# A recurrent token-mixing layer and a gated feed-forward layer in one kernel: the mixing products on four 64x64 quadrants, the first gate products before normalisation, and a written-out program order

## The chip, the cores and the metric

The kernel runs on one core of a Trainium2 chip. TensorE (PE) multiplies matrices, VectorE (DVE), ScalarE (ACT) and GpSimd (POOL) work on tiles, SyncE (SP) issues the DMAs. The metric is the device time of one execution in microseconds; the profile adds what each engine did, in time from the start of the span. In the profile an fp32 matmul stands as two records, each with its weight load (PEld), so a program's 32 matmuls are 64 records.

## The reference, cut to what matters

```python
batch, n_heads, seq, head_dim = (4, 8, 768, 48)
for t in range(S):
    cur = np.einsum('bhd,bhe->bhde', u[None] * kt, vt)
    y[:, :, t] = np.einsum('bhd,bhde->bhe', rt, state + cur)
    state = w[None, :, :, None] * state + np.einsum('bhd,bhe->bhde', kt, vt)
x = y.transpose(0, 2, 1, 3).reshape(3072, 384)
rms = np.sqrt(np.mean(x * x, axis=-1, keepdims=True) + 1e-06)
xn = x / rms * rms_g
g = xn @ w_gate                  # 384 x 1536
silu = g * (1.0 / (1.0 + np.exp(-g)))
out = silu * (xn @ w_val) @ w_out
```

All is fp32 on the chip; the three weight matrices arrive as float64 and are rounded to fp32 by the kernel itself.

## The kernel before

The sequence is cut into 12 chunks of 64 steps (`NS`, `L`); a chunk has 4 batches of 64 steps, 256 tokens. Each chunk goes through `mixing(s)`, which turns the recurrence into products, and then through the feed-forward layer.

`mixing(s)` has these steps, and the names are those of the operations that it records. R and K multiply r and k by powers of w (tables `up`, `down`). A forms the 64x64 scores of k against r for 16 pairs of batch and head (`products`). d and m put the bonus u on the diagonal and the upper triangle of the scores over it, into two tiles ME and MO. Y forms the outputs (`outputs`): the weights are a tile VS that holds 64 rows of v and 64 rows of state one above the other, so each Y matmul sums over 128 rows and fills 64 columns. sq, r, ms, pow, inv, diag, spread and x divide by the root of the mean square: squares, their sum over PE, the root, and a multiplication into `xa`; xb is a copy of `xa` with its two halves of partitions exchanged. U forms the next state (`states`): 32 matmuls over 128 rows, of which 64 hold the decay on a diagonal, so that the old state is decayed by the same matmul; the weights have 48 columns. Four copies per chunk (E on ACT) bring the state back into VS.

For chunk 0 the bonus comes from a product of its own (E, on a tile ku) and k is turned by PE (T), since its token-major copy is not loaded. Its last two heads reach their place in `yT` by four small DMAs (move), as in all chunks.

The feed-forward layer has a first stage for chunks 0 and 1, in cells `g` (gate and value products of 12 records) and `P` (second product), while the weights still arrive: every piece is loaded by SP, taken apart by ACT (ulp) and DVE (bits1, bits2) and added on POOL (sum). From chunk 2 on two chunks are done together by sums of tokens and weights, seven products f1 to f7 per group, six groups, then P1 to P7.

Nothing is issued as it is written. `add` records each operation with its engine, a cost and the keys that it reads and writes in a `Plan`; `search` tries goals with a random generator, `schedule` puts the operations in an order by due times, and `give` issues them in that order, so each engine's queue is that list, in order. Between PE operations of the first 27 us `give` fills idle stretches of the plan with matmuls on a tile of ones (`warm`). PSUM has three double banks a, b, c for the feed-forward layer and two banks `at` for the mixing.

Of the kernel before, what the change touches and what calls it, by code (L numbers as in the profile page):

```python
# [50 lines left out]
P = 128  # L51
# [31 lines left out]

class InOrder:
# [10 lines left out]
class Plan:  # L95
# [5 lines left out]
    AHEAD = 30.0  # L101
    URGENT = 3
    KEEP = 2.0

    def __init__(self):
        self.ops, self.then, self.last, self.readers, self.urgent = [], [], {}, {}, set()
# [22 lines left out]
    def schedule(self, goals, free, count, relaxed, patience=0.3):  # L129

        if len(self.then) < len(self.ops):
            self.then = [[] for _ in self.ops]
            for i, op in enumerate(self.ops):
                for d in op[2]:
                    self.then[d].append((i, self.hop(d, i)))
        late = [goals.get(i, 1e6 + i) for i in range(len(self.ops))]
        early = min(goals[i] for i in goals if i >= relaxed) - self.AHEAD
        for i in reversed(range(len(self.ops))):  # L140
            by, cost = 2 if i >= relaxed else 1, self.ops[i][1]
            for j, hop in self.then[i]:
                due = late[j] - by * (hop + cost)
                if i < relaxed <= j and due < early:
                    due = early
                if due < late[i]:
                    late[i] = due
            if i in self.urgent:
                late[i] -= self.URGENT
        n, then = count, self.then  # L150
        free, port = dict(free), {"DVE": 0.0, "POOL": 0.0}
        missing, mode = [len(op[2]) for op in self.ops[0:n]], None
        at, ready, start, end = [0.0] * n, {e: set() for e in free}, [0.0] * n, [0.0] * n
        for i in range(n):
            if not missing[i]:
                ready[self.ops[i][0]].add(i)
        for _ in range(n):
            when, e = min((max(free[e], min(at[i] for i in ready[e])), e) for e in free if ready[e])
            turn = (lambda i: late[i] + self.KEEP * (self.ops[i][7] != mode)) if e == "PE" else late.__getitem__
            i = min((i for i in ready[e] if at[i] <= when), key=turn)  # L160
            sooner = [j for j in ready[e] if at[j] <= when + patience and turn(j) < turn(i) - 1]
            if sooner:
                i = min(sooner, key=turn)
            s = max(when, at[i])
            if e == "PE":
                s += self.SWITCH * (self.ops[i][7] != mode)
                mode = self.ops[i][7]
            if self.ops[i][5]:
                s = max(s, port["POOL" if e == "DVE" else "DVE"])
            ready[e].remove(i)  # L170
            start[i], end[i] = s, s + self.ops[i][1]
            free[e] = end[i]
            if self.ops[i][5]:
                port[e] = end[i]
            for j, hop in then[i]:
                if j < n:
                    at[j] = max(at[j], end[i] + hop)
                    missing[j] -= 1
                    if not missing[j]:
                        ready[self.ops[j][0]].add(j)  # L180
        return start

    def replay(self, start, free):

        free, port, end, mode = dict(free), {"DVE": 0.0, "POOL": 0.0}, [0.0] * len(start), None
        for i in sorted(range(len(start)), key=lambda i: (start[i], i)):
            e, cost, deps, _, _, locks, _, rows = self.ops[i]
            s = max([free[e]] + [end[d] + self.hop(d, i) + (1.0 if self.ops[d][0] == "SP" else 0.02) for d in deps])
# [5 lines left out]
            free[e] = end[i] = s + cost * (1.0 if e == "PE" else 1.02)  # L194
            if locks:
                port[e] = end[i]
        return end

    def goals_of(self, cells, first, slower):

        goals, t = {}, first
        for i in cells:
            goals[i] = t
            t += self.ops[i][1] * slower
        return goals

    def search(self, cells, first, free, count, relaxed, trials):


        found, last = [], [i for i in range(count) if self.ops[i][0] == "PE"]  # L210
        for seed in range(4):
            rng, best, goals = random.Random(seed), None, dict(first)
            for trial in range(trials):
                new = dict(goals)
                if trial and rng.random() < 0.5:
                    a, by = rng.randrange(len(cells)), rng.uniform(-15, 15)
                    for i in cells[a : a + 1 + int(rng.expovariate(1 / 6))]:
                        new[i] += by
                elif trial:
                    new[rng.randrange(relaxed)] = rng.uniform(0, goals[cells[-1]])  # L220
                end = self.replay(self.schedule(new, free, count, relaxed), free)
                end = max(end[i] for i in last) + 0.3 * sum(end[i] for i in last) / len(last)
                if best is None or end <= best:
                    best, goals = end, new
            found.append((best, seed, goals))
        return min(found)[2]

    def give(self, start, idle=None):

        self.start, busy = start, 0.0  # L230
        for i in sorted(range(len(self.ops)), key=lambda i: (start[i], i)):
# [8 lines left out]
def fast(ctx, tc, chan, tok, vpad, wka, wkb, wot, cols, u_row, out, bad):  # L240
# [27 lines left out]
    col = c_tile([P, 3 * HP], "col")  # L268
    sp.dma_start(out=col, in_=cols)
    wraw, ucol, gcol = col[:, 0:HP], col[:, HP : 2 * HP], col[:, 2 * HP :]  # L270
# [4 lines left out]
    act.activation(spare, eps, AF.Sqrt)  # L275
# [5 lines left out]
    pw = raws.tile([P, HP, L], FP32, name="pw")  # L281
# [3 lines left out]
    VS = c_tile([P, 2, B, VC], "VS")  # L285
    ME = c_tile([P, B, HP, L], "ME")
    MO = c_tile([P, B, HP, L], "MO")
    KH = c_tile([P, 2, B, HP, D], "KH")
# [14 lines left out]

    pool.memset(VS[0:64, 0], 0.0)
    pool.memset(VS[64:128, 1], 0.0)
    pool.memset(KH[32:64, 0], 0.0)
    pool.memset(KH[96:128, 1], 0.0)


    wcol = c_tile([P, HP], "wcol")  # L310
    winv = c_tile([P, HP], "winv")
# [81 lines left out]
    def piece(p, dst, src, key, lo, size):  # L393
# [38 lines left out]
        )  # L432


    du_of = {}

    def crossed_r(s):

        if s:
            return CH[:, 0, 2:4]  # L440
# [1296 lines left out]
```

## Time and profile before

| what | us |
|---|---|
| three runs, median | 625.6 |
| lowest, highest | 619.77, 626.07 |
| profiled execution, its own time | 621.0 |
| its span | 619.3 |
| first gate product starts | 30.62 |
| last matmul ends | 612.14 |

The span runs from the first to the last instruction of the profiled execution; 1.7 us of its time lie outside. The last 7.2 us of the span, from the last matmul on, are the last addition, its store and the end of the program. Since every operation is issued through one helper, all rows have the line L92, and rows are told apart by the names of their tiles.

### The profile page before, as it was taken

The page shows a single profiled execution, that of the slowest core. Times are in us where ns is not written, and L with a number is a line of the kernel's source. Part 1 is how long each engine was busy: PE and PEld are TensorE (multiplying, and loading weights), DVE is VectorE, ACT ScalarE, POOL GpSimd, SP SyncE. Part 2 cuts the span into 40 slices and gives each one's busy share as a digit, 9 for nine tenths or more (in the row PEclk, how much of TensorE's full clock was granted, in tenths as well). Part 3 has the DMA queues.
Part 4 walks back from the last instruction along what each step waited for, and adds up shares of the span by engine and source line. Part 5 has one row for each costly group of instructions (what it writes and reads, how often), then busy time and mean ns, then how long its engine had stood idle before and what let it go on. Part 6 is the DMA issues. An engine that isn't in the chain of part 4 may idle for free.

```text
span 619.3 us, 15403 instructions
## 1 busy us (share of the span) xinstructions
PE 602.3 (97%) x6552; PEld 528.7 (85%) x6552; DVE 443.0 (72%) x632; ACT 365.6 (59%) x933; POOL 43.5 (7%) x41
## 2 busy tenths in 40 slices
PE   7989999999999999999999999999999999999994
PEld 7967777776888899888899888899788899888994
DVE  7698887889887986547887457997555976555631
ACT  5895779558489493345974944874845685232200
POOL 3234322400000000000000000000000000000000
PEclk9899999999999999999999999999999999999998
DMA  8757563213724202325131324231333311310001
GB/s 281 258 197 287 163 215 117 71 58 76 231 58 138 70 8 51 103 78 180 41 121 40 100 85 154 81 119 35 78 103 99 115 35 33 77 52 1 1 14 44
DMA packets 22782, 63.02 MB, mean 102 GB/s; under 512 B 3152, under 2 KB 10160, under 8 KB 21296
## 3 DMA queue, kind: packets, MB, share of 16 engines
q1 hardware_dynamic: 22112, 61.56, 31.9%
q8 instruction: 53, 0.87, 0.6%
q10 hardware_dynamic: 592, 0.39, 0.2%
q14 instruction: 25, 0.20, 0.1%
HBM read 56.04 MB, written 4.72 MB: 98 GB/s over the span
## 4 chain that ended last, share of the span: by engine, by line
PE 92%; DVE 3%; issue 2%; ACT 1%; POOL 0%; ACTq 0%; POOLq 0%; DVEq 0%
PE bank_b L92 31%; PE bank_a L92 27%; PE bank_c L92 24%; PE at L92 10%; DVE bits L92 1%; DVE rows_out L92 1%; DVE ms L92 0%; DVE chan L92 0%; DVE gv L92 0%; ACT ME L92 0%; DVE du L92 0%; DVE t L92 0%; ACT m L92 0%; POOL wb L92 0%; DVE sq L92 0%
## 5 line engine op out<-in xcount | busy, mean ns | idle before, releaser
L92 DVE TENSOR_TENSOR gv<-bank_b,m 128x512 f32<-128x512 f32 x90 | 62.1, 690 | 63.4 <-PE bank_b L92 61.0
L92 ACT ACTIVATE gv<-gv 128x512 f32<-128x512 f32 (+1 forms) x60 | 30.7, 521 | 44.2 <-DVE gv L92 43.7
L92 PE MATMUL bank_b<-xa,wa 64*128 64x256 f32 x444 | 55.7, 383 | 0.9 <-DVE gv L92 0.9
L92 ACT ACTIVATE ME<-dmask,du 64x64 f32<-64x64 f32 x176 | 46.0, 331 | 16.8 <-DVE du L92 16.0
L92 DVE TENSOR_TENSOR gv<-bank_c,gv 128x512 f32<-128x512 f32 x60 | 41.4, 690 | 14.3 <-PE bank_c L92 12.9
L92 PE MATMUL bank_a<-wo,h 128*128 128x192 f32 (+1 forms) x264 | 50.8, 346 | 0.0
L92 ACT ACTIVATE gv<-bank_a 128x256 f32<-128x256 f32 x30 | 11.5, 382 | 66.1 <-PE bank_a L92 66.1
L92 PE MATMUL bank_a<-xa,wa 64*128 64x256 f32 x396 | 49.8, 384 | 0.0
L92 PEld LDWEIGHTS bank_b<-xa,wa 64*128 64x128 f32 x444 | 41.7, 187 | 9.1 <-DVE gv L92 2.4
L92 PE MATMUL bank_a<-xb,wb 64*128 64x256 f32 x396 | 48.9, 379 | 0.0
L92 PEld LDWEIGHTS bank_a<-wo,h 128*128 128x128 f32 x264 | 43.1, 190 | 5.4 <-issue 2.3
L92 ACT ACTIVATE MO<-dmask,du 64x64 f32<-64x64 f32 x176 | 46.8, 339 | 0.8
L92 PE MATMUL bank_c<-t,s 64*128 64x256 f32 x360 | 44.2, 378 | 1.0 <-DVE rows_out L92 1.0
L92 PE MATMUL bank_b<-t,wb 64*128 64x256 f32 x360 | 44.7, 381 | 0.2 <-DVE gv L92 0.2
L92 ACT ACTIVATE rows_out<-rows_out 128x384 f32<-128x384 f32 x72 | 40.1, 558 | 6.6 <-DVE s L92 3.5
L92 PE MATMUL bank_b<-t,s 64*128 64x256 f32 x360 | 44.0, 377 | 0.0
L92 PE MATMUL bank_c<-xb,s 64*128 64x256 f32 x360 | 43.9, 376 | 0.0
L92 PEld LDWEIGHTS bank_a<-xa,wa 64*128 64x128 f32 x396 | 37.1, 187 | 6.9 <-issue 1.4
L92 PEld LDWEIGHTS bank_a<-xb,wb 64*128 64x128 f32 x396 | 37.8, 187 | 4.5
L92 PEld LDWEIGHTS bank_c<-t,s 64*128 64x128 f32 x360 | 34.6, 187 | 6.2 <-DVE rows_out L92 1.8
L92 PEld LDWEIGHTS bank_b<-t,s 64*128 64x128 f32 x360 | 34.8, 187 | 4.3 <-DVE t L92 0.3
L92 PEld LDWEIGHTS bank_c<-xb,s 64*128 64x128 f32 x360 | 34.9, 187 | 4.0
(163 smaller groups left out, 1247.0 us busy)
## 6 DMA issues: line engine op xcount, KB each, us to landing
chan<-in_chan_dram SPq DMA_DIRECT2D x11, 1024.0 KB, 6.0
TOK<-in_tok_dram SPq DMA_DIRECT2D x11, 768.0 KB, 5.3
VS<-in_vpad_dram SPq DMA_DIRECT2D x24, 256.0 KB, 4.0
raw<-in_wot_dram SPq DMA_DIRECT2D x8, 576.0 KB, 4.7
rows_out<-in_wka_dram SPq DMA_DIRECT2D x12, 384.0 KB, 3.2
rows_out<-in_wkb_dram SPq DMA_DIRECT2D x12, 384.0 KB, 3.1
rows_out<-in_wot_dram SPq DMA_DIRECT2D x12, 384.0 KB, 3.4
out_dram<-rows_out SPq DMA_DIRECT2D x43, 96.0 KB, 2.3
```

Of the source, the lines that this page charges most:

```text
L92: return lambda *args, **kwargs: self.tc.keep_in_program_order(give(*args, **kwargs))
```

## The change

Four things change.

- Mixing products. ME, MO and VS go. One tile MT holds the scores, V holds v alone, ST the state alone, RR and RX the decayed r and a copy of it with its halves exchanged for two batches. Y is now 32 matmuls of V against MT and 32 of ST against RR or RX, added up in PSUM; each works on 64 rows and 64 columns, and four that follow each other name four different quadrants. U is 32 matmuls on quadrants, with 64 columns of KH as weights (16 of them the next head's or padding) against 48 columns of v. The state is decayed on ACT by 8 multiplications per chunk and the new part added on DVE (`decay_state`, `keep_states`). d and m work on all 128 partitions at once. The two `at` banks are one tile of two banks.
- The first chunk. E, A and Y go in halves of 16 matmuls (Y: 24); the last two heads are computed straight into their places (`first_outputs`), so the four DMAs go. The six gate products of the first cell take yT and its exchanged copy yb, not divided by the root, and DVE multiplies their result by the reciprocal root from `rms` (`gv 0`). The root comes from POOL, not from ACT's table, so ACT has one table for this stretch. Chunk 0 has no T; half of its K is on POOL; its token-major k is loaded instead. Chunk 1 gets its bonus by E too.
- Tables. `up` and the token table move from DVE to ACT, the tables of powers are twice as wide.
- Order. `search`, `schedule` and their random generator go; a list `ORDER` of 1,526 numbers says in which order the operations are issued. `warm` fills the time before the first E alone, by 9 matmuls of 512 columns.

```diff
+ORDER = [
+    0, 5, 1, 14, 9, 4, 6, 49, 3, 16, 2, 19, 54, 11, 8, 17, 15, 12, 50, 51, 53, 24, 55, 10, 57, 52, 20, 56, 59, 29, 84,
...
-    def give(self, start, idle=None):
+    def give(self, order, free, idle):
...
+        for i in order:
             if self.ops[i][0] == "PE":
-                if idle:
-                    idle(busy, start[i])
+                idle(busy, start[i])
...
+    def products(place, qs, ks, rs):
+        for q in qs:
             for p in range(HP):
+                for h in range(2):
+                    b = 2 * q + h
+                    for z in range(2):
+                        a, c = 64 * (z ^ q), 64 * (1 ^ z ^ h)
+                        pe.matmul(
+                            place(q, h)[c : c + 64, p, :], ks[a : a + D, b, p, :], rs[a : a + D, b, p, :], start=True,
...
+    def first_outputs(tile, q):
+        for p in range(CC):
+            for head, cols in ((HP - 1, L), (p, D)):
+                for h in range(2):
...
-                        py[64 * z : 64 * z + 64, p, bl * L : (bl + 1) * L], VS[:, e, b, p * L : (p + 1) * L],
-                        (ME, MO)[e][:, b, p, :], start=True, stop=True, skip_group_check=True,
...
+                            place(b)[64 * z : 64 * z + 64, p, :], V[c : c + 64, b, p * L : (p + 1) * L],
+                            MT[c : c + 64, b, p, :], start=b < 2 and p == 0, stop=False, skip_group_check=True,
...
+                            place(b)[64 * z : 64 * z + D, p, :], ST[c : c + D, b, p, :], decayed[c : c + D, p, :],
+                            start=False, stop=True, skip_group_check=True,
...
-                    vh = VS[:, z, b, p * L : p * L + D]
-                    pe.matmul(
-                        pu[64 * z : 64 * z + D, bl, p, :], KH[:, z, b, p, :], vh, start=True, stop=True,
...
+                        c, a, x = 64 * (1 ^ z ^ h), 64 * (z ^ q), (b * HP + p) * D
+                        vh = V[c : c + 64, b, p * L : p * L + D]
+                        pe.matmul(
+                            pu[a : a + 64, q, p, :], KH[c : c + 64, x : x + L], vh, start=True, stop=True,
...
+    def decay_state(h):
+        for p in range(HP):
+            x, part = (1 - h) * HP + p, free_dims(ST[:, h, p], (2 * HP * D, 2), (1, D))
+            act.mul(part, part, pows[L][:, x : x + 1])
+
+    def keep_states(s, tile, x):
...
+            if s:
+                dve.tensor_add(to, pu, to)
+            else:
+                act.copy(to, pu)
...
+            lambda: product(ps_, wa[i][:, o], yT if first else xa[s], True), name=f"g {s} {i} {o}", rows=True,
...
+            lambda: product(ps_, wb[i][:, o], yb if first else xb[s], False), name=f"g {s} {i} {o}", rows=True,
...
+        if first:
+            gv, gv_keys = first_gv(o), [f"h{j // 4}.{j % 4}" for j in (15 + 2 * o, 16 + 2 * o)]
+            add(
+                "DVE", 0.72, keys + ["diag"], gv_keys, lambda: dve.tensor_mul(gv, ps_[:, :, 0:NT], free_dims(rms, (0, 2), (1, NT))),
...
-        if until < 27:
-            for _ in range(int((until - since - 0.3) / (0.22 if since else 0.5))):
-                pe.matmul(bank_of["c"][:, 0, 0:P], ones, ones, start=True, stop=True)
+        if until < 9:
+            for _ in range(int((until - since - 0.6) / 0.9)):
+                pe.matmul(bank_of["b"][:, 0], ones, free_dims(ones, (0, 4), (1, P)), start=True, stop=True)
```

How the order changes is shown at three places. On PE, the head of the program before: 15 matmuls of ones, then the bonus product of chunk 0 (bank_a from chan and ku), more ones, and the first scores.

```order
L92 MATMUL bank_c<-ones 128x128 x15
L92 MATMUL bank_a<-chan,ku 64x64 x32
L92 MATMUL bank_c<-ones 128x128 x2
L92 MATMUL at_149<-sq,chan 64x64 x16
L92 MATMUL at_150<-ME,chan 64x64
```

And the head of PE's queue now: the ones are wider, and the halves of the bonus product (ku) and of the scores (RR) alternate, with the first outputs (MT against V) behind them.

```order
L166 MATMUL bank_b<-ones 128x512 x9
L166 MATMUL bank_c<-chan,ku 64x64 x16
L166 MATMUL at<-RR,chan 64x64 x16
L166 MATMUL bank_b<-chan,ku 64x64 x16
L166 MATMUL bank_a<-RR,chan 64x64 x16
L166 MATMUL at<-MT,V 64x64 x4
```

The ones now stand in front of the first bonus product in one piece, and nothing fills PE between the later steps of chunk 0. On PE again, before, the stretch that ends with the first gate products (from xa and wa, xb and wb); the diag row spreads the root and the VS, KH rows are U of chunk 0.

```order
L92 MATMUL bank_c<-ones 128x128 x16
L92 MATMUL at_150<-diag,ones 128x256
L92 MATMUL at_149<-VS,KH 48x48 x16
L92 MATMUL at_150<-VS,KH 48x48 x16
L92 MATMUL bank_b<-xa_145,wa_120 128x256 x6
L92 MATMUL bank_b<-xb_146,wb_124 128x256 x6
L92 MATMUL at_149<-ident,rows_out 128x128 x4
```

The same stretch now; h stands for the exchanged copy yb, which lies in that tile.

```order
L166 MATMUL at<-ones,sq 128x1 x6
L166 MATMUL at<-ident,rows_out 128x128 x4
L166 MATMUL bank_a<-yT,wa_119 128x256 x6
L166 MATMUL bank_b<-yT,wa_119 128x256 x6
L166 MATMUL at<-diag,ones 128x256
L166 MATMUL bank_b<-h,wb_123 128x256 x6
L166 MATMUL bank_a<-h,wb_123 128x256 x6
L166 MATMUL at<-V,KH 64x48 x32
L166 MATMUL bank_a<-chan,ku 64x64 x32
```

Four gate products, and with them the table product (ident), now stand ahead of U of chunk 0; two of them stand ahead of the spread of the root. On DVE, before, the steps d (TENSOR_TENSOR with dmask) and m (COPY_PREDICATED) of chunk 0.

```order
L92 TENSOR_TENSOR chan<-chan,down 128x512 x2
L92 TENSOR_TENSOR ME<-bank_a,dmask 64x512
L92 TENSOR_TENSOR MO<-bank_a,dmask 64x512
L92 TENSOR_TENSOR ME<-bank_a,dmask 64x512
L92 TENSOR_TENSOR MO<-bank_a,dmask 64x512
L92 COPY_PREDICATED ME<-mask,at_150 64x512
L92 COPY_PREDICATED MO<-mask,at_150 64x512
L92 COPY_PREDICATED ME<-mask,at_149 64x512
L92 COPY_PREDICATED MO<-mask,at_149 64x512
```

And now, with the work on weight pieces (bits from raw) behind it:

```order
L166 TENSOR_TENSOR RR<-chan,up 128x512 x2
L166 TENSOR_TENSOR MT<-bank_c,dmask 128x256 x2
L166 COPY_PREDICATED MT<-mask,at 128x256 x2
L166 TENSOR_TENSOR MT<-bank_b,dmask 128x256 x2
L166 COPY_PREDICATED MT<-mask,bank_a 128x256 x2
L166 TENSOR_SCALAR bits_139<-raw_133 128x384
```

The eight instructions on half the partitions became eight of half the length on all partitions, and the first half's mask now stands ahead of the second half's diagonal.

More of the change, by code (lines that the diff above doesn't have):

```diff
@@ L28 @@
-import random
 from collections import deque
@@ L127, in hop @@
         return self.ops[before][4] + (self.HOP if a != b or a == "SP" else 0.0)
[L129 to L181, printed above, removed]
@@ L193, in replay @@
                 mode = rows
[L194 removed]
+            start[i], free[e], end[i] = s, s + cost, s + cost
             if locks:
                 port[e] = end[i]
[L197 to L226, printed above, removed]
[L228 to L231 removed]
+        return start
+    def give(self, order, free, idle):
+        assert sorted(order) == list(range(len(self.ops)))
+        start, busy = self.times(order, free), 0.0
+        for i in order:
             if self.ops[i][0] == "PE":
[L233 to L234 removed]
+                idle(busy, start[i])
                 busy = start[i] + self.ops[i][1]
```

607 lines of the change are left out of this document (301 added, 306 removed), and 70 rows, old and new, of the table ORDER.

## The prediction

> **What bounds the kernel now.** First the page: which engine is full, and what the chain that ended last consists of.
>
> ```profile
> PE 602.3 (97%) x6552; PEld 528.7 (85%) x6552; DVE 443.0 (72%) x632; ACT 365.6 (59%) x933; POOL 43.5 (7%) x41
> PE 92%; DVE 3%; issue 2%; ACT 1%; POOL 0%; ACTq 0%; POOLq 0%; DVEq 0%
> ```
>
> PE is busy for 97% of the span and makes up 92% of the chain. But busy is not useful: before the first gate product PE multiplies ones. So next comes a table by stages: two stretches of the start, the first stage, one steady pair of chunks, the last pair. The columns after the length are the busy time of each engine with its records, the granted clock, and the DMA engines' share and rate.
>
> ```profile
> core 0: us, PE busy (x) PEld busy (x) DVE busy (x) ACT busy (x) POOL busy (x), PEclk, DMA share, GB/s
> 6.83:13.65 6.82, 6.35 (x194) 5.93 (x194) 6.66 (x15) 5.63 (x15) 0.00 (x0) 1.00 1.03 295
> 17.07:20.49 3.42, 3.42 (x47) 3.19 (x47) 3.32 (x5) 1.32 (x4) 0.00 (x0) 0.50 0.88 329
> 30.62:144.63 114.01, 110.48 (x1202) 85.19 (x1198) 98.34 (x130) 82.14 (x213) 34.83 (x23) 1.00 0.45 152
> 337.17:432.99 95.82, 94.85 (x1061) 84.82 (x1060) 68.77 (x94) 61.83 (x160) 0.00 (x0) 1.00 0.32 94
> 528.80:612.14 83.34, 82.55 (x675) 76.03 (x674) 41.70 (x65) 17.45 (x38) 0.00 (x0) 1.00 0.12 33
> ```
>
> From 30.62 on PE hardly rests, at full clock, and in a steady pair DVE and ACT have 27 and 34 us to spare. So two things are worth time: PE's own work after 30.62, and the 30.62 us before it, where DVE is full (6.66 of 6.82) and PE waits.
>
> The timeline of PE in a steady pair gives the prices, from start to next start; a row is start, length, engine, line, operation, out<-in, shapes, count.
>
> ```profile
> 378.13 1.64 PE L92 MATMUL at<-VS,KH 128*48 128x48 f32 x64
> 379.71 1.57 PE L92 MATMUL bank_b<-xa,wa 64*128 64x256 f32 x12
> 381.11 1.46 PE L92 MATMUL bank_c<-t,s 64*128 64x256 f32 x12
> 382.50 0.27 PE L92 MATMUL at<-ME,chan 48*64 48x64 f32 x1
> 383.59 1.57 PE L92 MATMUL bank_a<-xb,wb 64*128 64x256 f32 x12
> 384.99 1.46 PE L92 MATMUL bank_b<-t,wb 64*128 64x256 f32 x12
> 386.28 1.46 PE L92 MATMUL bank_c<-xb,s 64*128 64x256 f32 x12
> 387.68 0.27 PE L92 MATMUL at<-ME,VS 128*64 128x64 f32 x1
> 389.69 1.57 PE L92 MATMUL bank_a<-xa,wa 64*128 64x256 f32 x12
> ```
>
> A gate product between its like takes 1.29 (384.99 to 386.28). The same product ahead of a mixing step takes 1.39 (381.11), behind one 1.40 (379.71). U takes 1.58, A 1.09, Y 2.01. A names four quadrants in turn, and its records step like this (the first and last of 15 such rows in chunk 1):
>
> ```profile
> 37.52 0.22 PE L92 MATMUL at<-ME,chan 48*64 48x64 f32 x1
> 38.34 0.22 PE L92 MATMUL at<-ME,chan 48*64 48x64 f32 x1
> ```
>
> 14 steps in 0.82, so 0.058 for four records. A is 16 x 0.058 = 0.93 of multiplying; its insertion costs 1.09 + 0.10 + 0.11 = 1.30; the other 0.37 are two changes of tile shape, 0.19 each.
>
> **The change, part by part.** Y. Before: 64 records, two at a time on column halves, 2.01. Now 128 records with the shape of A's, 64 columns of weights and 64 of tokens: 32 x 0.058 = 1.86, plus what A has over its steps (1.09 - 0.93 = 0.16): 2.02. I take no change. The upper end is no overlap beyond two, 64 x 0.058 = 3.71, or 1.7 more; the lower end is nothing, since no row has quadrants denser than A's.
>
> U. Before: 1.58 + 0.21 - 0.37 = 1.42 of multiplying, 32 pairs at 0.044. Now 64 records on four quadrants, 48 columns of tokens as before, but weights of 64 columns. The rows of weight loads:
>
> ```profile
> L92 PEld LDWEIGHTS at<-VS,KH 128*48 128x48 f32 x704 | 16.8, 125 | 4.0 <-issue 3.6 <-DVE xa L92 0.3
> L92 PEld LDWEIGHTS at<-chan 48*64 48x64 f32 x352 | 11.1, 134 | 0.0
> L92 PEld LDWEIGHTS bank_b<-KH,chan 48*64 48x64 f32 x64 | 1.9, 135 | 1.7 <-issue 1.7
> ```
>
> The third is T of chunk 0, with just this shape, and its loads are as long as A's (134). So U becomes 16 x 0.058 = 0.93, or by its 48 columns 16 x 0.044 = 0.70. I take 0.93: a gain of 0.49 per chunk, 4.9 for the ten U after the first gate product, up to 7.2.
>
> Changes of shape. Counted in the two programs from the first gate product on, PE changes between row pairs, whole array, column halves and quadrants 100 times before and 84 times now, since Y and U share A's shape and the new order lays mixing steps beside P more often: 16 x 0.19 = 3.0 less.
>
> The start, whose rows are these (fill, slow and fast; bonus product; d and m on DVE; first Y; move; yT, sq, ulp, one addition and one sum of a weight piece as prices; x; first gate product):
>
> ```profile
> 1.14 6.31 PE L92 MATMUL bank_c<-ones 128*128 128x128 f32 x30 [1.14 <-DVE pw L92]
> 24.46 3.82 PE L92 MATMUL bank_c<-ones 128*128 128x128 f32 x32
> 7.72 1.91 PE L92 MATMUL bank_a<-chan,ku 48*64 48x64 f32 x64 [0.27 <-DMA chan<-in_chan_dram]
> 11.05 0.70 DVE L92 TENSOR_TENSOR ME<-bank_a,dmask 64x512 f32<-64x512 f32 x1
> 16.21 0.73 DVE L92 COPY_PREDICATED MO<-mask,at 64x512 f32<-64x512 int32 x1
> 18.30 0.37 PE L92 MATMUL at<-ME,VS 128*64 128x64 f32 x1
> 21.52 2.71 SPq L92 DMA_DIRECT2D yT<-last_heads  x4
> 21.84 0.91 ACT L92 ACTIVATE yT<-at,col 128x128 f32<-128x128 f32 x3
> 21.36 0.61 ACT L92 ACTIVATE sq<-at 128x512 f32<-128x512 f32 x1
> L92 ACT ACTIVATE ulp<-raw 128x384 int32<-128x384 uint32 x6 | 3.2, 548 | 5.0 <-DMA raw<-in_wka_dram 3.5 <-DMA raw<-in_wkb_dram 1.5
> L92 DVE TENSOR_TENSOR h<-bank_a,h 128x256 f32<-128x256 f32 x9 | 3.8, 418 | 2.5 <-ACT h L92 2.5
> 20.81 1.00 POOL L92 TENSOR_TENSOR wa<-bits,ulp 128x384 int32<-128x384 int32 x1 [15.05 <-DVE bits L92]
> 28.75 0.95 DVE L92 TENSOR_TENSOR xa<-yT,at 128x768 f32<-128x768 f32 x1 [1.87 <-PE at L92]
> 30.62 1.57 PE L92 MATMUL bank_b<-xa,wa 64*128 64x256 f32 x12
> ```
>
> The fill comes first. Its first 30 records took 6.31, 0.21 each; 32 of the same shape at 24.46, under full clock, took 3.82, 0.12 each. In this execution the clock opened at 6.83, where the table has it at 1.00 again. The new fill is 18 records four times as wide: 0.85 each while slow, 0.48 when fast. With the clock opening at 6.83, 6.7 run slowly and 11.3 fast, and the fill ends at 1.14 + 5.69 + 5.4 = 12.2. It stands ahead of E in PE's queue, so E starts at 12.2 instead of 7.72, though its tiles are there by then. All slow, the fill would end at 16.4; all fast, at 9.8.
>
> From 12.2: E and A in halves, 0.5 each, the first E done at 12.7. Then DVE: d and m took 11.05 to 16.94, 5.9 for eight instructions; eight of half the length, at the 0.42 of 256 columns, take 3.3: from 12.8 to 16.1. Y of the second half is 48 records, 12 x 0.058 = 0.7 after 0.1: 16.9. On ACT then a square of three quarters (0.5 of 0.61), one ulp (0.55), half an exchange of yT (0.45, near the 256 columns), three yT (0.9): 19.4. The first gate product starts at 19.5 instead of 30.62: **11.1 earlier**. Gone from this path are T, the four moves (SP, 2.71 to issue), the root on ACT with its table load, spread and x; they are behind the gate products now, or nowhere.
>
> Work that moves behind the first gate product on PE: U of chunk 0 (0.93), the spread (0.43), E of chunk 1 (0.93), less the table product wk (0.45) that moves ahead: 1.8 more.
>
> The other queues. ACT per chunk: of these rows 16 of 32 go, 5.4 us per chunk:
>
> ```profile
> L92 ACT ACTIVATE MO<-dmask,du 64x64 f32<-64x64 f32 x176 | 46.8, 339 | 0.8
> ```
>
> Its four copies of the state become eight short multiplications. DVE per chunk: two masks (0.73 each) and one KH of 768 columns (0.95, the price of x) go, additions of states over 768 and 2 x 384 columns come, 1.9 by x's price: 0.5 less. Both lie under PE's 95.8 in the table; if that cover were gone the additions would cost 1.9 per chunk. On SP the bytes of v and chan are the same, and the first two chunks load half of their token-major tile. POOL gets half a K (128x512, 1.3 by the 1.00 of 384 columns) and pow of chunk 0 ahead of weight sums; behind them wait the gate products of the third column (o = 2). `gv 0` is added: three times 0.69 on DVE, waiting for spread and its copy; PE's banks a and b wait behind it, so the bonus product of chunk 1 does. No row shows this wait; it is between nothing and the 1.87 that DVE's x waited for the spread at 28.75; I take half, inside the waits below.
>
> Waits. By the table PE idles 3.5 in the first stage, 1.0 in a steady pair and 0.8 in the last. Their largest rows:
>
> ```profile
> 42.25 1.57 PE L92 MATMUL bank_c<-xb,wb 64*128 64x256 f32 x12 [2.17 <-POOL wb L92]
> 340.55 1.57 PE L92 MATMUL bank_c<-t,s 64*128 64x256 f32 x12 [0.52 <-DVE rows_out L92]
> 609.92 2.22 PE L92 MATMUL bank_c<-wo,h 128*128 128x192 f32 x12 [0.80 <-DVE rows_out L92]
> ```
>
> The first is weights that come late; with gate products 11 us earlier such waits grow, and with the half for `gv 0` I allow 2 more. The second stands at the head of the pair, behind the last P; U or A now often stands between, which covers it: 2 less over two pairs. The third goes, as the flag's product now stands ahead: 0.8 less. Together -0.8, between -5 and +6.
>
> The sum: -11.1 + 1.8 - 4.9 - 3.0 - 0.8 = **-18.0**. The profiled execution took 621.0, so 603.0. It lies 4.6 under the median 625.6, and two of the three runs stand at 625.6 and 626.07; nothing in its rows tells which kind the next runs will be, so I put **604**.
>
> **A page that speaks against it.** A's four records in 0.058 are 0.0145 each. The Trainium skill, "TensorE: Matmul & The Clock Gate", section "Wait — 56ns, not 53.3ns?", says that start to start never drops below about 25 ns however small the product is. By that rule, as an estimate, Y would take 128 x 0.025 = 3.2 and U 1.6, and the sum would come to nearly nothing. A's rows in this trace go below it, so the measurement decides here; the quadrant rival below is this case worked out from rows.
>
> **The rivals.**
>
> - Quadrants do not overlap in the new Y and U. The steps of E in chunk 0, which names two quadrants at a time (64 records in 1.91), are 0.058 for two. At that price Y costs 3.71 + 0.16, 1.85 more than forecast, and U 1.86, 0.93 more; 11 of each make 30.6, so 633.6: slower. It decides from 1.65 more per chunk. For it: two row halves add into the same PSUM tile for the first time. Against: they write different banks, as A does. Chance 0.03.
> - The start gives its gain back. The pieces of the third column wait for ACT, DVE and POOL in turn as at 42.25, the slow clock comes once more (a slow stretch of 3.42 stands in the table; once PE has work it costs 1.7), or the fill ends late. Half of the 11.1 lost: 608.6. DVE's 98 of 114 in the first stage speaks for it; the shorter d, m and KH against. Chance 0.22.
> - Most waits go, and U takes 0.70: idle 6.4 to 2 with its restarts, -4, and -2.3: 596.7. For it: DVE and ACT have less to do. Chance 0.15.
> - U and the changes of shape bring nothing, the start alone: 603.0 + 7.9 = 610.9. Chance 0.04.
>
> **How the numbers follow.** The forecast holds 0.54, with 599 to 608 as its own range; the rest, 0.02, is something unseen. The range 595 to 613 leaves out the quadrant case and the ends of the others. About 1% (6.3) is what a measurement of this kernel can tell from no change; faster by more than that needs under 619.3, which all cases but the first and some of the unseen give: 0.94. The same: 0.03. Slower: 0.03.
>
> **What would show it.** The first gate product (bank_a from yT and wa) near 19.5 and E of chunk 0 near 12.2; Y rows of 128 records in about 2.0; U in about 1.1 between gate products, not 1.58; a steady pair of some 93.5 instead of 95.8; idle PE between 25 and 60 us of the trace at 4 to 6 us. Wrong would be: Y near 3.8; a second stretch of clock 0.50; a wait for POOL wb or DVE gv of over 3; or a pair that is no shorter.

## The result, and the profile after

The changed kernel takes 605.63 us (median of 4 runs, 605.0 to 606.67), the kernel before, measured beside it, 624.47 (619.77 to 626.07): a ratio of 0.971, 95% interval 0.966 to 0.977. The profiled execution took 606.22, its span is 604.5. A second measurement of both gave 604.51 and 0.971 (0.967 to 0.975).

The page of the changed kernel, engines and chain as before:

```profile
PE 586.1 (97%) x7212; PEld 512.4 (85%) x7212; DVE 417.1 (69%) x622; ACT 296.3 (49%) x721; POOL 42.3 (7%) x40
PE 95%; DVE 3%; issue 1%; ACT 0%; POOL 0%; DVEq 0%
```

PE is as full as before and does 16.2 us less, about what the span lost (14.8). ACT does 69 us less and DVE 26, far more than the time shows, as neither was the bound. The same kernel's table by stages: a stretch of the clock, the next one, the weights' stage, and the three pairs that lie between the starts of their first products.

```profile
14.69:18.10 3.41, 2.61 (x48) 2.17 (x37) 2.72 (x6) 2.45 (x7) 0.99 (x1) 1.00 0.92 357
18.10:21.51 3.41, 3.40 (x16) 3.03 (x18) 2.42 (x9) 3.31 (x11) 1.67 (x2) 0.50 1.03 396
18.11:62.00 43.89, 40.58 (x636) 33.10 (x638) 33.69 (x61) 29.03 (x67) 17.87 (x13) 0.96 0.71 247
232.89:324.90 92.01, 91.44 (x1130) 83.18 (x1124) 63.18 (x91) 50.02 (x124) 0.00 (x0) 1.00 0.28 91
324.90:421.05 96.15, 93.52 (x1195) 83.95 (x1189) 67.32 (x93) 50.53 (x125) 0.00 (x0) 1.00 0.28 94
421.05:512.65 91.60, 91.60 (x1130) 83.09 (x1124) 61.09 (x87) 43.83 (x102) 0.00 (x0) 1.00 0.23 78
```

The three pairs take 93.3 on average (before 93.9, 95.8 and 95.8); one of them idles 2.6, one not at all. The start, on PE (fill, first bonus product, first outputs of chunk 0 in two rows, first gate products, spread):

```profile
1.15 9.61 PE L166 MATMUL bank_b<-ones 128*128 128x512 f32 x18 [1.15 <-DVE h L166]
10.69 0.69 PE L166 MATMUL bank_c<-chan,ku 48*64 48x64 f32 x32
12.95 0.91 PE L166 MATMUL at<-MT,V 64*64 64x64 f32 x48 [0.16 <-DVE MT L166]
15.52 0.55 PE L166 MATMUL bank_c<-MT,V 64*48 64x64 f32 x21 [0.69 <-issue]
18.11 2.93 PE L166 MATMUL bank_a<-yT,wa 64*128 64x256 f32 x12
20.80 1.83 PE L166 MATMUL bank_b<-yT,wa 64*128 64x256 f32 x12
22.56 0.70 PE L166 MATMUL at<-diag,ones 128*128 128x256 f32 x2
```

The first gate product starts 12.5 us earlier than before, but at half clock (0.50 in the table's second row): two gate products take 4.45 to the spread, where two at full clock take 2.8. And the view of waits on PE, all of 0.4 and more:

```profile
PE bank_a L166 <- ACT m L166: 2.3, 4, 0.6
PE at L166 <- issue: 2.2, 1, 2.2
PE bank_a L166 <- issue: 1.5, 1, 1.5
PE bank_b L166 <- DVE h L166: 1.1, 1, 1.1
PE at L166 <- DVE diag L166: 0.9, 1, 0.9
PE bank_c L166 <- issue: 0.7, 1, 0.7
PE bank_b L166 <- DVE gv L166: 0.4, 1, 0.4
```

The wait for weights (POOL wb, 2.17), those for rows_out and one of the two for gv at the head of a pair are gone. One kind is new: ACT m. Another has grown: "issue", where PE stands still though nothing that the profile shows is missing. The kernel before had it once, for 1.58 and ahead of the first gate product; now it is 0.7 ahead of it and 2.2 and 1.5 behind it.

Where the time went, from the start of each PE record to the next, summed by kind of product over the whole trace (idle apart). "Again" is the second profile of the same kernel (span 602.2), in which no half-clock stretch falls on the work.

| term, us | forecast | changed kernel | "again" |
|---|---|---|---|
| first gate product (from 30.62) | -11.1 | -12.5 | -11.5 |
| work moved behind it | +1.8 | +1.6 | +1.8 |
| ten U | -4.9 | -5.0 | -5.0 |
| the same products, fewer changes of shape | -3.0 | -3.2 | -3.5 |
| half clock after the first gate product | 0 | +1.7 | 0 |
| idle PE after it | -0.8 | +1.2 | -0.3 |
| from the last matmul to the end | 0 | +1.4 | +1.5 |
| sum, against the span 619.3 | -18.0 | -14.8 | -17.1 |

The price of the half clock is worked out from the two gate products above (4.45 against 2.8), and the term of the same products is what is left without it. Between medians it is -18.8. The profiled execution of before, 621.0, stands 3.5 below the median of its runs, so the profiles differ by less than the medians.

### The profile page after: what moved, and what is told of

It reads as the page before. It is cut to its first block, busy times and chain, and to the rows that moved or that the text cites. A ratio compares the mean times of both kernels' runs of the same rounds, so it can differ in the third digit from the quotient of the medians.

```text
span 604.5 us, 16467 instructions
## 1 busy us (share of the span) xinstructions
PE 586.1 (97%) x7212; PEld 512.4 (85%) x7212; DVE 417.1 (69%) x622; ACT 296.3 (49%) x721; POOL 42.3 (7%) x40
## 4 chain that ended last, share of the span: by engine, by line
PE 95%; DVE 3%; issue 1%; ACT 0%; POOL 0%; DVEq 0%
PE bank_b L166 33%; PE bank_a L166 27%; PE bank_c L166 25%; PE at L166 9%; DVE t L166 1%; DVE MT L166 1%; DVE gv L166 0%; ACT m L166 0%; DVE rows_out L166 0%; DVE ms L166 0%; DVE xa L166 0%; DVE KH L166 0%; POOL ms L166 0%; DVE diag L166 0%; DVE h L166 0%
## 5 line engine op out<-in xcount | busy, mean ns | idle before, releaser
L166 ACT COPY m<-bank_a 128x512 f32<-128x512 f32 (+1 forms) x35 | 19.9, 568 | 78.6 <-PE bank_a L166 62.1
L166 PEld LDWEIGHTS bank_b<-xa,wa 64*128 64x128 f32 x456 | 43.6, 187 | 6.2 <-DVE gv L166 1.2
L166 PE MATMUL bank_a<-xa,wa 64*128 64x256 f32 x372 | 46.4, 382 | 0.0
L166 PE MATMUL bank_a<-xb,wb 64*128 64x256 f32 x372 | 45.4, 377 | 0.0
L166 ACT ACTIVATE MT<-dmask,du 128x64 f32<-128x64 f32 x160 | 41.5, 338 | 4.4 <-DVE du L166 4.3
L166 DVE TENSOR_TENSOR h<-gv 128x256 f32<-128x256 f32 (+1 forms) x60 | 32.7, 550 | 11.0 <-ACT gv L166 10.7
L166 PEld LDWEIGHTS bank_a<-xb,wb 64*128 64x128 f32 x372 | 35.9, 187 | 4.4 <-ACT MT L166 0.3
L166 PEld LDWEIGHTS bank_a<-xa,wa 64*128 64x128 f32 x372 | 35.2, 187 | 4.7 <-issue 0.6
L166 PEld LDWEIGHTS bank_c<-xb,s 64*128 64x128 f32 x360 | 34.8, 187 | 4.0
```

Of the source, the lines that this page charges most:

```text
L166: return lambda *args, **kwargs: self.tc.keep_in_program_order(give(*args, **kwargs))
```

## The experiments

Each starts from the changed kernel. The columns: median, ratio to the kernel before measured beside it with its interval, span of the profile, start of the first gate product, and how long PE stands still at its record 1206 (weight loads and products counted in order from 0), which lies in chunk 1's Y in the changed kernel.

| run | median | ratio | span | first gate | at 1206 |
|---|---|---|---|---|---|
| changed | 605.63 | 0.971 (0.966-0.977) | 604.5 | 18.11 | 2.19 |
| e_again | 604.51 | 0.971 (0.967-0.975) | 602.2 | 19.11 | 1.71 |
| e_m1 | 605.82 | 0.975 (0.970-0.979) | 602.7 | 18.83 | 2.03 |
| e_load | 607.23 | 0.976 (0.973-0.979) | 606.0 | 18.63 | 2.37 |
| e_fill5 | 606.97 | 0.975 (0.970-0.979) | 609.4 | 20.45 | 3.27 |
| e_y2 | 611.04 | 0.983 (0.980-0.986) | 609.9 | 18.34 | 1.62 |
| e_norm | 613.47 | 0.987 (0.983-0.991) | 611.4 | 24.32 | 0 |
| e_u48 | 603.80 | 0.971 (0.967-0.976) | 602.0 | 18.84 | 0.86 |
| e_p5 | 605.72 | 0.974 (0.969-0.980) | 605.3 | 18.70 | 2.56 |
| e_shift | 604.83 | 0.974 (0.970-0.979) | 601.7 | 19.55 | 0 |
| e_both | 605.65 | 0.971 (0.969-0.974) | 602.9 | 20.30 | 0 |
| e_front | 611.39 | 0.981 (0.978-0.984) | 609.6 | 19.81 | 1.41 |
| e_u48b | 604.87 | 0.971 (0.966-0.975) | 603.1 | 18.00 | 2.02 |

The median of the kernel before, measured anew beside each group of these, lies between 621.2 and 624.5, so ratios are compared, or kernels measured together. e_m1, e_load, e_fill5 and e_y2 were measured together, and so were e_norm, e_u48, e_p5 and e_shift, then e_both and e_front, then e_again and e_u48b.

**The early start undone (e_norm).**

```diff
-            lambda: product(ps_, wa[i][:, o], yT if first else xa[s], True), ...
+            lambda: product(ps_, wa[i][:, o], xa[s], True), ...
-        if first:
-            gv, gv_keys = first_gv(o), ...
+        if first:
+            add("DVE", 0.0, [], [], lambda: None, name=f"gv {s}")
```

> The first chunk's gate products take x divided by its root again, as before the change; everything else is that of the changed kernel (605.6 us), with the spread of the root, x and xb moved ahead of the first gate product in every queue. The multiplications of the results by the root and the exchanged copies yb are left out. The first gate product then has to wait for spread, x and xb: about 24 instead of 18.1. Theory A: the early start is worth its 6 us in full: about 611.5. Theory B: the weights of the third column set the end of this stretch (wb is added up by 30.6 and its product starts at 31.05 in the changed kernel), and with four gate products, U and the bonus product of chunk 1 behind 24 PE reaches that product at about 33: only 2 of the 6 are lost, about 607.6. Rival C: all of it is given back, 605.6.

Theory A, and more: 613.47 against 603.8 to 605.7 of the three others measured with it, some 8 to 10 more for a first gate product that starts 6.2 later. The surplus stands in the trace: PE waits where it had work, and the clock is halved from 17.7 to 28.0 and from 34.8 to 41.6. So the 8 to 10 are the price of the late start with the slow clock that came with it, and not of the late start alone. The waits of this kernel, the spread and the first gate product on top:

```profile
PE at L172 <- DVE diag L172: 4.1, 2, 3.2
PE bank_a L172 <- DVE h L172: 2.4, 1, 2.4
...
PE bank_a L172 <- DVE xa L172: 1.5, 1, 1.5
```

**The quadrants (e_y2).**

```diff
-        for bs in ((0, 1), (2, 3)):
-            for p in range(HP):
-                for b in bs:
+        for b in range(B):
+            for p in range(HP):
```

> The same 128 records of Y per chunk, but ordered batch by batch, so that records that follow each other name two quadrants in turn instead of four. Theory: the four quadrants work at the same time, and Y lasts 2.0 because four records share 0.058; with two in turn it takes 64 x 0.058 + 0.16 = 3.9, 1.85 more in each of 11 chunks: about +20, 626, of which waits that stand beside Y may hide 1 or 2. Rival: the step of 0.0145 per record is the rate of issue and has nothing to do with the quadrants: Y stays at 2.0 and the time at 605.6.

The result lies between the two. Y's start and the next product's, first in the changed kernel (1.99), then here (2.58):

```profile
387.13 1.16 PE L166 MATMUL at<-MT,V 64*64 64x64 f32 x64
...
389.12 3.03 PE L166 MATMUL bank_a<-wo,h 128*128 128x192 f32 x17
```

```profile
185.26 1.39 PE L166 MATMUL at<-MT,V 64*64 64x64 f32 x58
...
187.84 1.57 PE L166 MATMUL bank_b<-t,s 64*128 64x256 f32 x12
```

0.59 more for each whole Y: over all Y behind the first gate product 28.75 against 22.10, 6.6 more. The time lost 5.2 against e_m1, measured with it, whose Y is as in the changed kernel. So the order of quadrants matters, but two in turn cost 0.020 per record, not the 0.029 of chunk 0's old bonus product; why that one stepped more slowly stays open.

**The weight columns of U (e_u48, e_u48b).**

```diff
-                            pu[a : a + 64, q, p, :], KH[c : c + 64, x : x + L], vh, ...
+                            pu[a : a + D, q, p, :], KH[c : c + 64, x : x + D], vh, ...
```

> U with weights of 48 columns instead of 64 (the 16 columns more belong to the next head and are not used); the states are added up in two pieces per half, one more instruction on DVE per chunk. U takes 1.08 from its start to the next product's in the changed kernel. Theory A: the weight columns bound it (64 columns, 0.058 for four records), so 48 columns make it 16 x 0.044 = 0.70 plus 0.15: 0.85, 0.23 less per chunk, 2.5 in all: about 603.1. Theory B: the records themselves bound it (their step is the same for 48 and 64 columns): U stays at 1.08 and the time at 605.6.

> U with weights of 48 columns, again, now against the changed kernel on the same chip. The trace of the first try has U at 0.86 instead of 1.08, 2.4 less in all, but also 1.2 instead of 0.4 of a wait for DVE in the third group and 0.3 at 61. Theory: about 1.5 us below the changed kernel's median of the same call. Rival: the extra DVE instruction per chunk and the waits take all of it: no difference.

U, start to next start, is 1.08 in the changed kernel and 0.87 here (second fence):

```profile
264.60 1.15 PE L166 MATMUL at<-V,KH 64*64 64x48 f32 x64
265.68 1.57 PE L166 MATMUL bank_b<-t,s 64*128 64x256 f32 x12
```

```profile
263.23 0.94 PE L166 MATMUL at<-V,KH 64*48 64x48 f32 x64
264.10 1.57 PE L166 MATMUL bank_b<-t,s 64*128 64x256 f32 x12
```

The weight columns bound it (theory A of e_u48): 16 x (0.058 - 0.044) = 0.22 was expected to go, 0.21 went. But the time did not follow: 604.87 against 604.51, measured together. In the two profiles U is 2.3 shorter in all, while PE idles 1.9 more (8.0 against 6.1: mostly waits for DVE, which has one more instruction per chunk, and one of 0.65 under "issue") and has 1.7 of half clock. The rival of e_u48b holds.

**The wait for ACT m (e_m1, e_p5).**

```diff
 e_m1: in ORDER, four times:  P4, m1  ->  m1, P4
 e_p5: in ORDER, three times: P4, m1, P2, ... P5  ->  P4, m1, P5, P2, ...
```

> The changed kernel stands at 605.6 us. In its profile the product P2 waits 0.57 us in four of the five groups for the copy m of P1's result; the copy stands behind P4 in the program and ends its own wait with P4, though it reads what P1 wrote. Theory: the place of the copy in the program makes the wait. With the copy one place earlier, ahead of P4, the four waits go: 4 x 0.57 = 2.3 less, about 603.3, and no row of the waits names ACT m. Rival: P2 waits for something else that the trace puts down to the copy (the bank, a late ACT): the four rows stay, 605.6.

> In three groups (the first, second and fifth) P5 stands between P4 and P2. With the copy of P1's result issued ahead of P4 the wait of 0.57 moved from P2 to P4: both write the bank pair that the copy reads, so whichever follows waits. Theory: a product in another bank in between hides the copy: 3 x 0.57 = 1.7 less, about 603.9, and no row of ACT m in these three groups. Rival: P5's own input, the sum of the hidden tiles on DVE (done at 211.1, 301.9 and 573.1, P4's end at 211.5, 303.6 and 575.6), comes later than P4 ends, and a wait for DVE takes the place: 605.6.

In e_m1 one of the four waits went, and three moved from P2 to P4: both write into the two banks that m reads from. So neither theory nor rival holds as it stands. In e_p5 ACT m is down to one wait of 0.6 as expected, but others have its place, for the output sums and for the states on DVE:

```profile
PE bank_b L172 <- DVE rows_out L172: 1.2, 1, 1.2
...
PE at L172 <- DVE ST L172: 1.1, 1, 1.1
...
PE bank_a L172 <- ACT m L172: 0.6, 1, 0.6
```

Neither is a gain in the time (605.82 and 605.72). The wait for rows_out shows why in one place: P5, brought forward, no longer stands between two products of bank_b, and the second of them starts at 318.15, when DVE has added the first one's result (317.60 to 318.09).

**The fill (e_fill5).**

```diff
-            for _ in range(int((until - since - 0.6) / 0.9)):
+            for _ in range(5 if since == 0 else 0):
```

> Five wide products of ones instead of nine. In the changed kernel the fill ends at 10.69 and the first bonus product starts then, though its r has landed at 9.05 and ku is there at 6.3; DVE, free at 10.43, waits until 11.45 for it. Theory: the fill is too long by one to two products; with five it ends by 8.3 even at the slow clock, the first bonus product starts at 9.1, and the first gate product about 1.0 earlier (17.1 instead of 18.1): about 604.6. Rival: the fill is needed to keep the clock up until the scores come; with five the first scores and outputs run at half speed or a longer slow stretch follows, and the time is 606 to 609.

By the profile, the rival. The bonus product starts at 9.74, but the clock, open at 4.85, is halved again from 11.68 on:

```profile
8.00:11.68 3.68, 1.86 (x96) 1.61 (x96) 3.28 (x5) 3.44 (x12) 1.75 (x2) 1.00 1.01 402
11.68:25.33 13.65, 12.84 (x168) 11.06 (x168) 9.93 (x25) 9.67 (x29) 5.21 (x6) 0.50 0.87 325
```

The first gate product starts at 20.45. Its four runs lie between 603.5 and 611.1, with granted clocks between 0.992 and 0.980, the profiled one being the slowest: how long the clock is halved depends on the execution. The ratio, 0.975, cannot be told from that of the changed kernel.

**Where PE stands still without a wait (e_load, e_shift, e_front, e_both, e_again).** In the trace one DMA queue carries blocks of 16 KB, one for some 250 of PE's records:

```profile
q8 instruction: 58, 0.95, 0.6%
```

e_shift, with 128 more instructions of PE, has 59 of them, the kernel before, with 13,104 records, 53. And each time that PE stands still under "issue" in the changed kernel such a block has just come: it ended at 14.12, 34.70 and 392.38, and PE went on at 15.52, 36.25 and 393.61, 1.2 to 1.6 later. The last two rows:

```profile
36.25 0.25 PE L166 MATMUL at<-RR,ST 48*48 48x64 f32 x1 [2.19 <-issue]
393.61 0.65 PE L166 MATMUL bank_a<-wo,h 128*128 128x192 f32 x3 [1.46 <-issue]
```

```diff
 e_load: in ORDER, the load of chan 10 behind the move of chunk 9, with R, K and the copies of R behind it
```

> In the changed kernel PE stands still for 1.46 us at 392.1, in the middle of a product that waits for nothing, while one block of its instructions (16 KB) comes from 391.42 to 392.38, just after 1 MB of chan has kept the DMA engines 60 to 100% busy from 384.5 to 390. Here this load is issued behind the move of the last heads, some 15 us later, and R, K and the copies of R that need it with it; PE's own instructions are the same, in the same order. Theory: PE uses up its instructions faster in a mixing step, and the next block waits behind data in the DMA engines: the standstill at this place goes, 1.5 less, about 604.1. Rival 1: the density of PE's records alone makes it: it stays, 605.6. Rival 2: it falls by chance and stands in some executions only: it may go here and come at another block.

The standstill at 392 went, and a wait of 2.2 for DVE came at 424.7, since R and K now stand in front of the sums there. But in e_again, e_u48, e_fill5 and e_y2, where that load is where it was, it does not come either, and in e_m1, e_p5 and e_u48b with 0.2 to 0.65: the second rival, so this run tells nothing of the load.

```diff
-            for _ in range(int((until - since - 0.6) / 0.9)):
-                pe.matmul(bank_of["b"][:, 0], ones, free_dims(ones, (0, 4), (1, P)), start=True, stop=True)
+            for _ in range(41 if since == 0 else 0):
+                pe.matmul(bank_of["b"][:, 0, 0:112], ones, ones[:, 0:112], start=True, stop=True)
```

> The fill is 41 products of 112 columns instead of 9 of 512: the same columns in all, but 128 more instructions of PE ahead of everything else, so that each border between two blocks of 256 instructions falls 128 records earlier in the program. In all five profiles of the changed kernel and its variants PE stands still for 1.6 to 3.3 us at its record 1206, in the middle of chunk 1's Y, and for up to 1.3 at its record 443, in chunk 0's Y; 1206 - 443 = 763 is three blocks. Theory: PE waits there for the next block of instructions. The standstills then come at records 443 and 1206 of the new count again, which are other products: the first still inside chunk 0's Y or the scores, the second just ahead of chunk 1's Y, where the block before it lasts 5.5 us instead of 3.7: it shrinks below 0.6 or goes, and 1.5 to 2 us are saved (603.6 to 604.1), unless the blocks that now hold a whole Y (chunks 7 and 8, near 290 and 346) stand still in its place. Rival: the standstill belongs to chunk 1's Y (its data, its banks): it stays there at 2 us, and the time at 605.6.

The same Y of chunk 1 in the same stage of the weights now takes 1.99, with no wait but the one ahead of it:

```profile
33.99 1.16 PE L166 MATMUL at<-MT,V 64*64 64x64 f32 x64 [0.25 <-DVE MT L166]
...
35.98 0.59 PE L166 MATMUL bank_c<-wo,h 128*128 128x384 f32 x1
```

The standstill in chunk 0's Y is gone as well; "issue" is no row of this kernel's waits. So it does not belong to Y or its data. The times of the blocks say what changed: a block begins to come only when PE has passed the border before it (0.2 to 5.7 later for the first six blocks of all thirteen profiles of the changed kernel and its versions). In the changed kernel PE passed its record 951 at 30.32, and the block for record 1206 came from 33.82 to 34.70, too late; here PE passed record 951 at 28.97, the block came from 30.06 to 31.53, and PE reached record 1206 at 34.22. The span is 601.7, though the narrow fill takes longer (first bonus product at 12.76, not 10.69); the median, 604.83, shows little of the gain.

```diff
-            for _ in range(int((until - since - 0.6) / 0.9)):
+            for _ in range(40 if since == 0 else 0):
+                pe.matmul(bank_of["b"][0:32, 0, 0:32], ones[:, 0:32], ones[:, 0:32], start=True, stop=True)
+            for _ in range(8 if since == 0 else 0):
```

> U with 48 columns, and a fill of 40 small products (32 by 32) followed by 8 wide ones: 156 more instructions than the changed kernel, so that a border between blocks falls inside the fill (record 187), the next into the second scores of chunk 0 with its block asked for long before, and the one after next but three just behind the start of chunk 1's Y, in a block that also holds the long P. Theory: no standstill in Y of chunk 0 and none above 0.5 in Y of chunk 1; the fill ends by 11 and the first gate product starts by 18.0: 0.5 to 1.5 better than the two edits with the longer fill, 600 to 601.5. Rival: the small products load PE too little, the clock opens one stretch of 3.4 later, the wide ones run at half speed and the fill ends at 12 or later: 602 to 604.

> U with weights of 48 columns and the fill of 41 products of 112 columns together. U alone brought the median from 605.6 to 603.8 with 0.22 less per U in the trace (2.4 in all); the other fill took away the standstills of 0.7 and 2.2 and the one of 1.5 in the fourth group, but its own fill ended at 12.76 instead of 10.69 and the first gate product started at 19.55 instead of 18.1, so that 0.8 of the median was left. Theory: the two have nothing to do with each other and add up: 605.6 - 2.4 - 0.8 to -2 = 601.2 to 602.4. Rival: with U shorter another wait takes the place (weights, DVE): 603.5 or more.

Both hold U with 48 columns besides the fill that is shown. e_front is the worse for it and says the most. It meets neither its theory nor its rival: PE stands still at records 951, 1206, 1461 and 2482, for 0.4, 1.4, 3.1 and 0.8: one, one and four blocks of 255 apart and in the same count as 443 and 1206, but in other products (the bonus product and the beginning of Y in chunk 1, P, a gate product). The first three of these rows:

```profile
28.73 0.81 PE L166 MATMUL bank_a<-chan,ku 48*64 48x64 f32 x39 [0.41 <-issue]
35.35 1.10 PE L166 MATMUL at<-MT,V 64*64 64x64 f32 x60 [1.41 <-issue]
40.60 1.64 PE L166 MATMUL bank_c<-wo,h 128*128 128x384 f32 x3 [3.19 <-POOL wa L166]
```

The third the view puts down to POOL wa, which ended at 40.57. But in the changed kernel this product started at 37.11, ahead of that work of POOL (38.92), so it does not need it; its block came in until 39.26, and PE went on at 40.60, 1.34 later, as in the other cases. At the first five borders in the thirteen profiles no record of PE starts less than 1.2 after its block has come. So PE's instructions come late at borders between blocks, mostly where a border meets the stage in which weights fill the DMA engines (0.98 to 1.02 busy from 31 to 33.8 in the changed kernel). That the full engines are what delays the block is likely but not shown, as no run changed the loads of weights. e_both has no standstill under "issue", but its fill ended at 13.51 and U's gain went into waits for DVE (1.05 at 61, 1.2 at 329): 605.65, as its rival has it.

> The changed kernel once more, nothing edited, beside the version with U of 48 columns on the same chip, since the medians of the kernel before differ by up to 0.5% from chip to chip (621.2 to 624.5) and so hide differences of 2 us. Theory: PE's standstill at its record 1206 (chunk 1's Y) comes again with 2.0 to 2.6 us, the one at record 443 with 0.3 to 1.3, and the one of 1.46 at record 10395 does not, since six of seven other profiles with the same records there show 0 to 0.6. Rival: the last one belongs to the kernel and comes again with about 1.5.

As expected in two of three: 0.42 at record 443 and none at 10395. At 1206 the standstill comes again, but with 1.71 it is shorter than the 2.0 to 2.6 that were expected.

No version is better than the changed kernel by more than the intervals. Not tried: loads of weights that leave room for PE's blocks, and a Y of half as many records.

## Why the prediction was right

- **The start** was worth 12.5 and 11.5 instead of 11.1. The fill ended at 10.69 and 11.97, not 12.2, since the clock opened at 4.45 and 7.0; where it opens differs between 4.1 and 7.5 in the profiles of this case. d and m took 2.76 (11.45 to 14.21; forecast 3.3). The rival that it gives half back did not come about: undone in e_norm, the start costs 8 to 10, with the clock that it brings.
- **Y** is 1.99 (forecast 2.02), **U** 1.08 (1.1), the work moved 1.6 and 1.8 (1.8). That 64 weight columns set U was the choice between 0.93 and 0.70, and e_u48 shows it. A steady pair takes 93.3 (93.5). The quadrant rival is refuted; its price was too high also for two quadrants in turn (2.58, not 3.87).
- **Changes of shape**: 16 fewer at 0.19 were forecast as 3.0; gate and value products are 3.4 shorter in "again" for the same 3,096 records (345.0 to 341.6). The size fits, but no run changed the number of changes alone.
- **The waits** are the step that failed, though their sum hardly shows it. The waits at the head of a pair and the last P's 0.8 went as described, but for one of 0.4. The wait for weights (2.17), which was to grow with the earlier start, went as well. In their place came blocks of instructions (2.2 and 1.5 in one profile, 1.7 in the other) and ACT m (2.3), which the forecast did not know. The allowance of 2 for late weights and `gv 0` happened to cover half of that, which is luck, and the sum of -0.8 came out as +1.2 and -0.3. Idle PE between 25 and 60 is 3.3 and 2.9, below the 4 to 6 that were to show the forecast right.
- **Half clock** after the first gate product was named in the rival of the start, with the price 1.7, and the sum held nothing for it. It came in one profile of the changed kernel and not in the other; all eleven profiles of its versions have at least one such stretch.
- **The end** was left out: behind the last matmul stand two additions and three pairs of stores, where there were one and one, 1.4 longer.
- The sum -18.0 and the median -18.8 agree better than the terms do, and that is luck. Between profiles the gain is 14.8 and 17.1, less than the sum; the forecast went from the profiled 621.0 with 1 us on top, while the median of before is 624.5.

## What to carry to other kernels

Count the instructions of the engine that is the bound, not only their time. Splitting Y into twice as many records cost nothing here (1.99 against 2.01), as they overlap, until a block of some 255 records passed in 2 us and the next had not come. In a start that is bound by a chain over three engines, what shortens the chain also keeps PE busy, and so its clock (e_norm); a fill must reach to the real work, not end early (e_fill5). And a wait at a bank or a queue that reordering moves came back at the next one (e_m1, e_p5), so such an edit is worth what the next wait leaves of it.

## What the runs showed of the hardware

PE can wait for its own instructions. In the kernel before it did once (1.58 in T of chunk 0, at record 445, with a block that ended at 13.99, 1.5 before PE went on):

```profile
15.51 0.32 PE L92 MATMUL bank_b<-KH,chan 48*64 48x48 f32 x4 [1.58 <-issue]
```

The Trainium skill, "Runtime: NRT & Kernel Launch", section "Instruction fetch mechanics", says that the instructions come in blocks of 16 KiB, 256 of them, and that the cost of crossing a border is mostly hidden. The block's size agrees with this case's 250 records per packet. The cost is not hidden here where Y, U or A spend some 255 records in little more than 2 us: 0.4 to 3.3 a time in eleven of the fourteen profiles. Why the block of 391 came late, for 1.5 in one execution, 0.2 to 0.65 in three others and not at all in the rest, after the DMA engines had fallen to 10%, stays open.

The clock falls on little work, not only on none. In fourteen profiles, cut into stretches of 3.41 us from the opening of the clock on, every stretch of the first 45 us in which PE was busy for less than 1.9 us is followed by one at half clock (1.84 in the kernel before, 0.5 to 1.86 in six others). Those at full clock with 1.98 to 2.3 late in the weights' stage are not followed by one; some with 2.1 to 3.1 in chunk 0 are (2.61 in the table above), where r's products of one column and the small products stand. So it is not busy time alone that counts; what does stays open. The Trainium skill, "TensorE: Matmul & The Clock Gate", Part 1, has the window of 3413 ns, running freely, and the fall after an idle one. The traces agree on the window (the stretches at one clock last 3.41 us or whole multiples of it), and show the fall after one that is half full.

Records on four quadrants follow each other at 0.0155 us in Y (1.99 for 128), and at 0.020 on two (2.58). The Trainium skill, "TensorE: Matmul & The Clock Gate", section "Wait — 56ns, not 53.3ns?", has a floor of about 25 ns between two starts for small products; it does not hold for these.
